# Partition counts of four kinds of DMA piece in a two-layer attention and long-convolution kernel

## The chip, the cores and the metric

The kernel runs on one core of a Trainium2 chip. A core has five engines that follow their own instruction streams: TensorE (PE, with weight loads listed as PEld), VectorE (DVE), ScalarE (ACT), GpSimd (POOL) and SyncE (SP). SP computes nothing here; it issues most of the DMA transfers, one after the other, and the 16 DMA engines of the core carry them out. SBUF, the on-chip memory, has 128 partitions (rows); a transfer names a range of partitions and what lies in each of them. The metric is the device time of one execution in microseconds (us), lower is better.

## The reference, cut to what matters

The input x has 2048 positions of 512 channels. Two kinds of layer alternate, A, B, A, B, each added to x:

```python
x = x + _A_ref(_layernorm(x), A_wqkv, A_wo)
x = x + _B_ref(_layernorm(x), B_A_re, ..., B_Dskip)
# and the same two once more, with the same weights
```

Layer A is a sliding, dilated attention: with 32 heads of 16 channels, position s attends to the eight positions s, s-2, ..., s-14:

```python
W, dil = 8, 2
idx = pos[:, None] - off[None, :]                     # off = 0, 2, ..., 14
logits = jnp.einsum("bhsd,bhswd->bhsw", q, kg) * scale
attn = _softmax(jnp.where(mask, logits, -1e9), axis=-1)
o = jnp.einsum("bhsw,bhswd->bhsd", attn, vg)          # then o @ wo
```

Layer B is a long convolution of every channel with a filter K made from the parameters, done as a Fourier product:

```python
Kf = rfft(pad(K)); Uf = rfft(pad(u))
y = irfft(Uf * Kf)[:L] + u * Dskip
```

## The kernel before, in words

Positions are stored with p as partition and a as column: position 16 p + a, so that 128 partitions times 16 columns hold all 2048. The residual stream x lies in `x_sb` as 128 x 16 x 512 bf16.

**Values and their shifted rows.** `v_ext` has 30 columns of 512 channels. Columns 14 to 29 hold the values of the 16 columns a. A position that looks back past column 0 needs the value of a higher column one partition earlier, so columns 0 to 13 repeat columns 16 to 29 shifted down by one partition. DVE's multiply L476 (`pv_mult`, tile `pav`) then reads eight columns in steps of two in one instruction. In `core`, `v_proj(a)` (L399 to L412) computes a column of values; the even columns come first (`VROWS`). After column 14, and again after column 15, SP copies the seven even or the seven odd shifted columns, from 127 source partitions to the 127 partitions below. Each such copy is two transfers: 112 partitions (L407) and 15 partitions (L408), of 7 x 1 KB each. In the first layer the event `("v", 0)` or `("v", 1)` follows: it calls `x_load`.

**Residual rows.** `x_load` (L1471) brings x from HBM into `x_sb`, four columns at a time, 128 partitions of 4 KB. It is called for block 0 after the even shift and for blocks 1 to 3 after the odd shift of the first layer. The output weights' loads (L312) stand before the first call on SP; behind the second stand the filter table's loads (`k_half_load`, L1374 and L1390, in two halves) and the first layer's twiddle loads. TensorE's output projection (L510, `out_proj`) reads `x_sb`.

**Twiddle pieces.** Layer B is a two-step Fourier transform. Its second step (`f2`, L828) multiplies with a twiddle matrix per frequency. `w2` is a list of 32 tiles of 128 partitions x 4 matrices x 128 (1 KB a partition), loaded from `w2_dram`. Their place is the memory of the attention layer's keys and projection weights (tile `kT_ext`, `homes` in L210), so they can only be loaded once the attention has read these. `load_w2(part)` (L595) issues eight loads; the letter `W` of the order strings `CORE0` and `CORE1` calls it, four times in each layer. The class attribute `self.layer` is 0 in the first pass and 1 in the second.

**What SP issues behind them in the second layer.** `FftB.run` calls `pump` (L756 and L758, in `kf_read`), which loads the filter's spectrum from `kf_dram` in 16 portions of three transfers each into a ring of buffers. Portions 0 to 6 are loaded during the attention, 7 to 9 right after the twiddle pieces, and each of 10 to 15 when DVE's product L865 (`u_mult`, tile `t`) has freed a buffer. Portion 7's place lies in the tile `kT_ext`, and its load waits until all twiddle loads have landed. The products run in the order of the portions, and the inverse transform of the second half needs all of them.

The order of instructions on DVE, ACT, PE and SP is written out by hand in strings such as `CORE1` and `ORDER1`; each engine works strictly in its order. SP's transfers use eight completion semaphores in turn, so a transfer waits until the one eight before it has landed.

Of the kernel before, what the change touches and what calls it, by code (L numbers as in the profile page):

```python
# [199 lines left out]
class LayerA:  # L200
# [162 lines left out]
    def core(self, x_sb, u, lnp, order, ev, nprod=0):  # L363

        tc, nc, lnst, l = self.tc, self.nc, self.lnst, self.layer
# [7 lines left out]
        with ExitStack() as c2:  # L373
            big = c2.enter_context(tc.tile_pool(name=f"a{l}_big", bufs=1, reuse_waits="tile"))
            v = big.tile([P, NA + 14, D], BF16, name="v_ext")
# [15 lines left out]
            def pq_tile():  # L391
                return ps_q.tile([P, 512], F32, name="pq", tag="pq")
# [6 lines left out]
            def v_proj(a):  # L399
                pp = pq_tile()  # L400
                for dt in range(NDT):
                    nc.tensor.matmul(pp[:], lhsT=xnT[:, dt, a * P:(a + 1) * P],  # L402
                                     rhs=wv[:, dt, :], start=(dt == 0), stop=(dt == NDT - 1))
                nc.scalar.copy(v[:, 14 + a, :].rearrange("p (d h) -> p d h", h=H), pp[:].rearrange("p (h d) -> p d h", h=H))  # L404
                if a >= 14:
                    b = a - 14
                    nc.sync.dma_start(v[1:113, b:14:2, :], v[0:112, 16 + b:30:2, :])  # L407
                    nc.sync.dma_start(v[113:128, b:14:2, :], v[112:127, 16 + b:30:2, :])  # L408
                    if b + l == 0:
                        self.load_wo(big)  # L410
                    if ("v", b) in ev:
                        ev["v", b]()  # L412
# [134 lines left out]
            def calls(f, *args):  # L547
                return [lambda a=a: f(*a) for a in args]

            def logit(f):  # L550
# [8 lines left out]
            rows = [(a,) for a in (ROWS1 if l else ROWS0)]  # L559
            ops = dict(  # L560
                m=calls(mult, *qft[nprod:]), l=calls(logit(lsum), *qft[nprod:]),
                q=calls(q_proj, *qft[len(self.qT) * NDT:]), v=calls(v_proj, *((a,) for a in VROWS)),
                x=calls(mx, *blocks), e=calls(sub_exp, *blocks), r=calls(recip, *blocks), n=calls(norm_p, *blocks), T=calls(turn, *blocks[:ncol]),
                P=calls(pv_mult, *rows), O=calls(out_proj, *rows[:15]), t=calls(x_stats, (12,), (13,)),
                b=calls(u_begin, (0, 4, "act", "pool"), (4, 8, "act", "act"), (8, 12, "act", "act")),
# [28 lines left out]

    def load_w2(self, w2_dram, part):  # L595
        for c in range(8 * part, 8 * part + 8):
            self.nc.sync.dma_start(self.w2[c], w2_dram[:, c * 4:(c + 1) * 4, :])  # L597

    def w2_loads(self, w2_dram):
        part = iter(range(4))  # L600
# [795 lines left out]
def kernel(  # L1396
# [16 lines left out]
    nc = tc.nc  # L1413
# [3 lines left out]
    w2_dram = dram.tile([P, P, P], BF16, name="w2_dram")  # L1417
# [14 lines left out]
    x_v = A_x.rearrange("b (p a) d -> p (b a) d", p=P)  # L1432
# [11 lines left out]
    x_sb = xpool.tile([P, NA, D], BF16, name="x_sb")  # L1444
# [25 lines left out]

    def x_load(bs):  # L1471
        for b in bs:
            nc.sync.dma_start(x_sb[:, b * 4:(b + 1) * 4, :], x_v[:, b * 4:(b + 1) * 4, :])

    with tc.tile_pool(name="ctmp_g2", bufs=1) as g2tmp:
        gx, ga, gs = build_g2(nc, g2tmp, C["p21"], g2_dram, kp[:].rearrange("p q a r -> p (q a r)"))
        G = lambda f, h: lambda: f(h)
        K = lambda h, j: lambda: k_part(h, j)
        for h in range(4):
            gx(h)  # L1480
        angled = iter(range(4))
        ev = {("v", 0): lambda: x_load((0,)), ("v", 1): lambda: x_load((1, 2, 3)),
              "c": lambda: ga(next(angled)), "1": lambda: k_half_load(0), "6": lambda: k_half_load(1),
              "2": G(gs, 0), "3": G(gs, 1), "4": G(gs, 2), "5": G(gs, 3),
              "7": lambda: nc.scalar.preload_act_table_set(EXP_LN),
              "8": lambda: k_half_fix(0), "9": lambda: k_half_fix(1)}
        ev |= la.w2_loads(w2_dram)
        ev |= {c: K(i // 4, i % 4) for i, c in enumerate("ABCDEFGH")}
        late = la.core(x_sb, u, lnp, CORE0, ev, 3)
# [121 lines left out]
```

## Time and profile before

| | us |
|---|---|
| median of three runs (389.51 to 390.7) | 390.63 |
| profiled execution | 390.38 |
| its span, first to last instruction | 387.9 |
| DVE busy | 369.0 (95%) |
| ACT busy | 338.1 (87%) |
| PE busy | 320.9 (83%) |
| POOL busy | 63.4 (16%) |

The granted TensorE clock over the span is 0.941 of full speed. The DMA engines moved 54.15 MB, 140 GB/s in the mean.

How to read what is shown below. A page gives, for one profiled execution, the busy time of each engine, a chain of work that ended last, groups of instructions, and DMA issues with the median time from issue to landing. A timeline row has start, duration, engine, source line, operation, output<-inputs and a count; `SPq` is SP's queue, and the duration of a DMA row there is the time that SP spends on issuing, not the time of the transfer. When several like instructions follow each other they are merged into one row, whose duration reaches from the first start to the last end. A row by source line gives minimum, median and maximum duration in ns, then the first and last start. The waits view lists who waited for whom: total us, times, longest. A window row gives the busy time of PE, PEld, DVE, ACT and POOL in that stretch, the granted clock, the DMA engines' mean busy share and GB/s.

### The profile page before, as it was taken

To read this page: it belongs to the slowest core of one execution; us is meant where nothing else is said; L and a number is where in the kernel's file an instruction comes from. 1 tells how busy PE (TensorE), PEld (TensorE's weight loads), DVE (VectorE), ACT (ScalarE), POOL (GpSimd) and SP (SyncE) were. 2 spreads that over 40 slices of the span, in tenths; PEclk is the share of its full clock that TensorE was granted. 3 is DMA by queue.
4 is the path that set the end of the run, shared out by engine and by line. 5 is a ranking of instruction groups with operands and counts; after the bars stand their busy time and mean duration, and the time that the engine had idled before them with its cause. 6 is when DMAs were issued, how large, how long until landed. Compare 5 with 4: busy or idle time off the path is not lost.

```text
span 387.9 us, 14510 instructions
## 1 busy us (share of the span) xinstructions
PE 320.9 (83%) x6312; PEld 220.8 (57%) x6361; DVE 369.0 (95%) x439; ACT 338.1 (87%) x581; POOL 63.4 (16%) x97
## 2 busy tenths in 40 slices
PE   3000277999999999999998999999999999997895
PEld 2000125757634455666887899553446676667895
DVE  6999999999999999999999989979999999989985
ACT  7999999898578799999999998865575889989994
POOL 9400980000190000101622200300000010000000
PEclk9555569999999999999999999999999999999999
DMA  7951822214026556487476733068305675003706
GB/s 208 398 178 17 86 74 68 43 29 88 25 71 172 153 183 191 107 232 214 183 276 240 272 113 111 3 230 259 96 0 136 189 211 167 4 3 106 224 25 196
DMA packets 68301, 54.15 MB, mean 140 GB/s; under 512 B 33545, under 2 KB 58670, under 8 KB 67982
## 3 DMA queue, kind: packets, MB, share of 16 engines
q1 hardware_dynamic: 66566, 48.70, 43.0%
q0 software_dynamic: 1664, 4.52, 3.2%
q8 instruction: 49, 0.80, 0.9%
q14 instruction: 14, 0.11, 0.1%
q10 hardware_dynamic: 8, 0.00, 0.0%
HBM read 30.15 MB, written 13.24 MB: 112 GB/s over the span
## 4 chain that ended last, share of the span: by engine, by line
PE 41%; ACT 22%; issue 4%; SPq 3%; DMA 2%; DVE 0%; ACTq 0%
PE pq L402 7%; ACT a1s L810 5%; PE pq L227 5%; ACT ub L877 5%; PE pp L286 3%; PE L L354 3%; PE po L501 3%; PE pq L512 2%; PE pb L821 2%; ACT xnT L195 2%; PE pb L891 2%; SPq L597 2%; PE pb L895 2%; PE pb L940 2%; PE L L428 2%
## 5 line engine op out<-in xcount | busy, mean ns | idle before, releaser
L476 DVE TENSOR_TENSOR pav<-attn,v_ext 128x4096 bf16<-128x4096 bf16 (+1 forms) x34 | 72.2, 2156 | 0.0
L346 DVE TENSOR_TENSOR prod<-qT,kT_ext 128x4096 bf16<-128x4096 bf16 x29 | 65.4, 2286 | 1.9 <-ACT qT L229 0.6
L1213 PE MATMUL pt<-ident,x_blk 128*128 128x128 bf16 x64 | 6.3, 241 | 40.1 <-ACT x_blk L195 40.1
L1127 DVE TENSOR_TENSOR A_t<-A_t,pow_t 128x1024 bf16<-128x1024 bf16 (+4 forms) x46 | 38.1, 868 | 0.1
L501 PEld LDWEIGHTS <-pav 64*128 64x128 bf16 x1984 | 31.1, 95 | 11.7 <-issue 5.8
L501 PE MATMUL po<-ident,pav 64*128 64x64 bf16 x1984 | 34.8, 190 | 0.3 <-issue 0.2
L512 PE MATMUL pq<-wop,oT 128*128 128x512 bf16 x120 | 31.3, 379 | 2.9 <-issue 2.1
L877 ACT CAST ub<-pb 128x1024 bf16<-128x1024 f32 x32 | 31.6, 1111 | 0.0
L828 PE MATMUL pb<-a1s,kT_ext 128*128 128x64 bf16 x768 | 27.7, 193 | 3.6 <-ACT a1s L810 1.9
L810 ACT CAST a1s<-pb 128x1024 bf16<-128x1024 f32 x30 | 29.4, 1052 | 1.4 <-PE pb L821 1.2
L402 PE MATMUL pq<-wv,xnT 128*128 128x512 bf16 x123 | 29.8, 379 | 0.3
L1223 PE MATMUL pp<-xnT,kT_ext 128*128 128x512 bf16 x89 | 25.5, 408 | 5.3 <-ACT kT_ext L1228 2.1
L1213 PEld LDWEIGHTS <-x_blk 128*128 128x128 bf16 x64 | 4.8, 108 | 42.4 <-ACT x_blk L195 41.2
L404 ACT CAST v_ext<-pq 128x512 bf16<-128x512 f32 x32 | 18.7, 587 | 11.1 <-PE pq L402 10.8
L828 PEld LDWEIGHTS <-kT_ext 128*128 128x128 bf16 x768 | 24.9, 98 | 6.0 <-issue 4.3
L1285 PEld LDWEIGHTS <-A_t 128*64 128x64 bf16 (+1 forms) x512 | 21.6, 103 | 3.8 <-DVE A_t L1127 0.2
L227 PE MATMUL pq<-xnT,kT_ext 128*128 128x512 bf16 x90 | 23.4, 380 | 0.4 <-issue 0.2
L1285 PE MATMUL pk<-B_t,A_t 128*64 128x84 bf16 (+1 forms) x512 | 23.5, 201 | 0.1
L810 DVE CAST a1s<-pb 128x1024 bf16<-128x1024 f32 x18 | 21.4, 1217 | 1.5 <-PE pb L821 1.1
L503 ACT CAST oT<-po 128x512 bf16<-128x512 f32 x31 | 17.8, 575 | 3.4 <-PE po L501 3.4
L402 PEld LDWEIGHTS <-xnT 128*128 128x128 bf16 x128 | 11.9, 98 | 15.5 <-issue 2.3
L512 PEld LDWEIGHTS <-oT 128*128 128x128 bf16 x128 | 12.5, 98 | 12.6
(262 smaller groups left out, 880.9 us busy)
## 6 DMA issues: line engine op xcount, KB each, us to landing
kT_ext<-w_dram SPq DMA_DIRECT2D x64, 128.0 KB, 3.5
w_dram<-xnT SPq DMA_DIRECT2D x1, 4096.0 KB
kf_ring<-kf_dram SPq DMA_DIRECT2D x13, 256.0 KB, 3.9
kf_ring<-kf_dram SPq DMA_DIRECT2D x26, 128.0 KB, 3.9
v_ext<-v_ext SPq DMA_DIRECT2D x4, 784.0 KB, 5.6
x_blk<-in_A_x_dram SPq DMA_DIRECT2D x4, 512.0 KB, 5.4
kT_ext<-in_A_wqkv_dram SPq DMA_DIRECT2D x4, 512.0 KB, 13.2
x_sb<-in_A_x_dram SPq DMA_DIRECT2D x4, 512.0 KB, 6.8
```

The lines of the kernel that those rows point to most:

```text
L227: nc.tensor.matmul(pq[:], lhsT=self.wqk[:, dt, ft * P:(ft + 1) * P], rhs=self.xnT[:, dt, q * 512:(q + 1) * 512], start=(dt == 0), stop=(dt ...
L346: nc.vector.tensor_tensor(pr, self.qT[q][:, ft].unsqueeze(1).to_broadcast([P, W, 4, P]), kap, ALU.mult)
L402: nc.tensor.matmul(pp[:], lhsT=xnT[:, dt, a * P:(a + 1) * P], rhs=wv[:, dt, :], start=(dt == 0), stop=(dt == NDT - 1))
L476: nc.vector.tensor_tensor(pv[:, i], attn[:, n % 4].unsqueeze(2).to_broadcast([P, W, DH // parts, H]), vap, ALU.mult)
L501: nc.tensor.matmul(po[:, h, 0, i * nt + ft, :], lhsT=pvf[rows, i, w, ft * P:(ft + 1) * P], rhs=ident[rows, rows], start=(w == 0 and ft + i ...
L512: nc.tensor.matmul(pw[:], lhsT=oT[:, ftp, :], rhs=self.wo[:, ftp, :], start=False, stop=(ftp == NDT - 1))
L810: (self.nc.scalar.copy if eng == "act" else self.nc.vector.tensor_copy)(dst, src)
L828: nc.tensor.matmul(p2[:, j, :], lhsT=self.w2[(ec * EC + j) // 4][:, j % 4, :], rhs=a1s[:, ec * EC + j, :], start=True, stop=True)
L877: nc.scalar.copy(ub[:], p2)
L1127: return lambda: nc.vector.tensor_tensor(*args)
L1223: nc.tensor.matmul(pps[kind, b, ft][:], lhsT=la.wqk[:, dt, c:c + P], rhs=la.xnT[:, dt, b * 512:(b + 1) * 512], start=(dt == 0), stop=(dt = ...
L1285: nc.tensor.matmul(o, lhsT=lhs, rhs=Bt[:, ri, c * CH + ql].rearrange("p b g -> p (b g)"), start=(not half and j % 4 == 0 and ri == 0), sto ...
```

## The change

Three places are changed. The shifted value rows go as 100 and 27 partitions instead of 112 and 15. In the second pass each twiddle tile is loaded as two pieces of 110 and 18 partitions instead of one of 128. The residual rows are loaded as 110 partitions per block, and the other 18 partitions once per call for all blocks of the call, so block 0 takes two transfers and blocks 1 to 3 take four. The bytes moved are the same.

```diff
-                    nc.sync.dma_start(v[1:113, b:14:2, :], v[0:112, 16 + b:30:2, :])
-                    nc.sync.dma_start(v[113:128, b:14:2, :], v[112:127, 16 + b:30:2, :])
+                    for lo, hi in ((1, 101), (101, 128)):
+                        nc.sync.dma_start(v[lo:hi, b:14:2, :], v[lo - 1:hi - 1, 16 + b:30:2, :])
...
     def load_w2(self, w2_dram, part):
         for c in range(8 * part, 8 * part + 8):
-            self.nc.sync.dma_start(self.w2[c], w2_dram[:, c * 4:(c + 1) * 4, :])
+            parts = (slice(0, 110), slice(110, 128)) if self.layer else (slice(0, 128),)
+            for p in parts:
+                self.nc.sync.dma_start(self.w2[c][p], w2_dram[p, c * 4:(c + 1) * 4, :])
...
     def x_load(bs):
         for b in bs:
-            nc.sync.dma_start(x_sb[:, b * 4:(b + 1) * 4, :], x_v[:, b * 4:(b + 1) * 4, :])
+            nc.sync.dma_start(x_sb[0:110, b * 4:(b + 1) * 4, :], x_v[0:110, b * 4:(b + 1) * 4, :])
+        rows = slice(4 * bs[0], 4 * bs[-1] + 4)
+        nc.sync.dma_start(x_sb[110:128, rows, :], x_v[110:128, rows, :])
```

## The prediction

> **What bounds the kernel now.** I read the page first (share of each engine, DMA issues), then SP's timeline, because the change only alters transfers that SP issues, then the DVE and weight-load timelines at the places that consume those transfers, and last SP's own waits.
>
> ```profile
> span 387.9 us, 14510 instructions
> ...
> PE 320.9 (83%) x6312; PEld 220.8 (57%) x6361; DVE 369.0 (95%) x439; ACT 338.1 (87%) x581; POOL 63.4 (16%) x97
> ...
> kT_ext<-w_dram SPq DMA_DIRECT2D x64, 128.0 KB, 3.5
> ...
> v_ext<-v_ext SPq DMA_DIRECT2D x4, 784.0 KB, 5.6
> ```
>
> DVE is busy 95% of the span, so in most stages it is the bound: a transfer that comes late to DVE costs its full lateness, one that comes in time costs nothing. The question is how much room each changed transfer has, and whether SP's queue, which works strictly in order, still has room behind them.
>
> The sum is made against the profiled execution: 390.38 us, of which 387.9 are the span and 2.5 lie around it. It stands 0.25 us below the median of three runs (390.63).
>
> **The shifted value rows.** SP's and DVE's timelines at the four shifts (two in each layer):
>
> ```profile
> 117.97 0.70 SPq L407 DMA_DIRECT2D v_ext<-v_ext  x1
> ...
> 130.04 0.64 SPq L407 DMA_DIRECT2D v_ext<-v_ext  x1
> ...
> 131.67 2.83 SPq L1473 DMA_DIRECT2D x_sb<-in_A_x_dram  x3
> ```
> ```profile
> 275.71 0.67 SPq L407 DMA_DIRECT2D v_ext<-v_ext  x1
> ...
> 292.17 0.64 SPq L407 DMA_DIRECT2D v_ext<-v_ext  x1
> ```
> ```profile
> 126.83 4.48 DVE L476 TENSOR_TENSOR pav<-attn,v_ext 128x4096 bf16<-128x4096 bf16 x2
> ...
> 139.08 2.28 DVE L476 TENSOR_TENSOR pav<-attn,v_ext 128x4096 bf16<-128x4096 bf16 x1
> ```
> ```profile
> 284.56 2.28 DVE L476 TENSOR_TENSOR pav<-attn,v_ext 128x4096 bf16<-128x4096 bf16 x1
> ...
> 301.23 4.49 DVE L476 TENSOR_TENSOR pav<-attn,v_ext 128x4096 bf16<-128x4096 bf16 x2
> ...
> 360.40 1.22 DVE L865 TENSOR_TENSOR t<-ub,kT_ext 128x2048 bf16<-128x2048 bf16 x1
> 361.54 2.35 DVE L865 TENSOR_TENSOR t<-ub,kx 128x2048 bf16<-128x2048 bf16 x2
> ...
> 364.94 2.35 DVE L865 TENSOR_TENSOR t<-ub,kf_ring 128x2048 bf16<-128x2048 bf16 x2
> ...
> 368.34 4.62 DVE L865 TENSOR_TENSOR t<-ub,kf_ring 128x2048 bf16<-128x2048 bf16 x4
> ```
> ```profile
> L408 SPq DMA_DIRECT2D v_ext<-v_ext x4: 898/932/963, 118.7 to 292.9; - x4
> ...
> DMA to landing us min/median/max: 5.1/5.3/5.5
> ```
>
> From the start of L407 to the multiply that reads the shift there are 8.86, 9.04, 8.85 and 9.06 us. Both pieces have landed after about 0.70 + 5.3 = 6.0 (L408 starts some 0.7 later), so each shift has 2.8 to 3.0 us to spare. What the copy does to the DMA engines shows in this window of the second layer, where little else moves:
>
> ```profile
> 278.00:279.00 1.00, 1.00 (x6) 0.42 (x5) 0.88 (x1) 0.98 (x2) 0.00 (x0) 1.00 0.96 260
> 279.00:280.00 1.00, 1.00 (x17) 0.55 (x15) 0.98 (x1) 0.76 (x2) 0.00 (x0) 1.00 0.99 295
> ```
>
> The last two columns are the DMA share and GB/s: 112 and 15 rows keep the 16 engines 96 to 99% busy. The 889 KB (784 + 105) take about 3.4 us of the 6.0 at 260 GB/s. How 100 and 27 rows spread, no row tells. Lower bound: as now. Upper bound: half the engines, 3.4 us more, and 9.4 is past all four dates by 0.4 to 0.6, in sum 1.9 us on DVE. I take nothing, since less than 2.8 of these 3.4 us is covered. [...]
>
> **The residual rows.** Four loads become six; the first pair stands in an idle stretch of SP before 130.04. In the second batch SP now needs 130.04 to 134.50 for five issues; six at L408's 0.93 plus 0.05 between two are 5.9, so SP comes out about 1.4 us later. If the engines' rate halved as well, the batch's 2.4 MB would take 8 us more, since the next queue entries wait for landings:
>
> ```profile
> SPq L1390 <- DMA x_sb<-in_A_x_dram: 3.2, 3, 2.0
> ```
> ```profile
> 182.09 0.37 SPq L1499 DMA_DIRECT2D g_sb<-g_dram  x1
> ...
> 189.52 1.17 SPq L853 DMA_DIRECT2D kT_ext<-kT_ext  x2
> ```
>
> SP runs without a pause through the filter loads and the first layer's twiddle loads and is first idle from 182.46 to 189.52: 7.1 us of room, which hides the 1.4. The upper end, 1.4 + 8, would overrun it by 2.3; the lower end is nothing. I take nothing, because the real spread must be much worse than the worst shift row to get there.
>
> **The second layer's twiddle pieces** are the large item: 32 loads become 64, behind one another in one queue.
>
> ```profile
> 301.34 16.72 SPq L597 DMA_DIRECT2D kT_ext<-w_dram  x29
> 320.64 0.52 SPq L756 DMA_DIRECT2D kT_ext<-kf_dram  x1
> ...
> 325.93 1.23 SPq L758 DMA_DIRECT2D kx<-kf_dram  x2
> 352.52 0.45 SPq L756 DMA_DIRECT2D kf_ring<-kf_dram  x1
> ...
> 363.30 0.54 SPq L756 DMA_DIRECT2D kf_ring<-kf_dram  x1
> 363.89 1.23 SPq L758 DMA_DIRECT2D kf_ring<-kf_dram  x2
> ```
> ```profile
> SPq L597 <- DVE prod L346: 4.6, 1, 4.6
> ...
> SPq L756 <- DMA kT_ext<-w_dram: 2.3, 1, 2.3
> ```
> ```profile
> 356.51 1.02 PEld L828 LDWEIGHTS <-kT_ext 128*128 128x128 bf16 x33
> ```
> ```profile
> L597 SPq DMA_DIRECT2D kT_ext<-w_dram x29: 320/430/1407, 301.3 to 317.6; - x29
> ...
> DMA to landing us min/median/max: 2.4/3.6/4.2
> ```
> ```profile
> L758 SPq DMA_DIRECT2D kf_ring<-kf_dram x12: 594/595/1452, 353.0 to 364.5; - x12
> ...
> DMA to landing us min/median/max: 2.6/3.7/5.5
> ```
> ```profile
> L407 SPq DMA_DIRECT2D v_ext<-v_ext x4: 637/654/699, 118.0 to 292.2; - x4
> ```
>
> Three loads go out early; the fourth waits 4.6 us for the last logit product and leaves at 301.34. From there 29 loads take 16.72 us, to 318.06. Now they are 58. Queued behind them on SP, in order: a wait for the last of them to land (320.64), nine filter loads for the seventh to ninth product (to 327.16), and six more triples that refill the ring for the tenth product and later ones. Today SP has 25 us of idle time before 352.52.
>
> How late may the twiddle loads end? Call the end E. The nine loads start at E + 2.6 and take 6.5. If SP is then behind, the six triples follow without a pause, 1.9 us each (363.30 to 363.84, 0.05, then 1.23, 0.05), so the last is issued at E + 20.6, its last piece starting 0.6 earlier and landing 3.1 after that (L758's pieces: 2.6 at least, 3.7 in the middle): E + 23.1. The last product starts at 368.34 + 3x1.15 = 371.8. So nothing is late while E stays under 348.7; past that each us of E costs a us. 58 loads from 301.34 reach 348.7 at 0.817 us each.
>
> The price of one piece decides. No row shows 110 or 18 rows. Lower bound: the 128-row load's 0.43 (0.48 with the gap), E = 329, cost nothing. 64-row pieces take 0.595 and 112 rows 0.654, while the 15-row piece, less data in the same form, takes 0.932: the issue is dear not by size but by the row count. Upper bound: twice the 15-row piece's extra (0.932 - 0.654 = 0.278) on top of the 64-row price, 1.15, or 1.20 with the gap: E = 370.9, cost 22.2 us. I take 0.932 + 0.05 = 0.98 for both, since 15 is the only count in the trace that isn't 16 or a multiple of it, as 110 and 18 aren't. E = 301.34 + 58x0.98 = 358.2, **9.5 us** past the date. The weight loads come in the same stretch: the last twiddle piece would land near 361 against its use about 357.4, 3.6 late, inside the 9.5 and not added. A gain from fewer bytes per engine at a time isn't excluded but has no path: everything that follows on SP has room today.
>
> [...]
>
> PE waits for two landings per twiddle tile instead of one: 32 more waits. Lower bound nothing, upper 32 times the 0.05 that a step between two issues costs on SP, 1.6 us; I take nothing, as PE stands idle in this stretch for other reasons. Bytes, matmuls, DVE and ACT work are unchanged.
>
> **Sum.** 390.38 + 0 (shifts) + 0 (residual rows) + 9.5 (twiddle queue) = 399.9 us.
>
> **Rivals.**
> - Not slower: the pieces are issued at 0.43 to 0.82 us. E stays under 348.7 and all is hidden, 390.4 us. It decides at 0.817 us a piece. For it: 128-row loads at 0.43. Against: the 15-row row. One piece at 0.43 and one at 0.93 would give 0.73 with the gaps, and so this case.
> - Dearer: odd counts cost more the further they are from 16. At 1.20 a piece the cost is 22.2, 412.6 us. For it: both new counts are further from a 16-way split than 15 is. Against: no row over 0.963 that isn't a stall.
> - The shifts bind: at half rate 1.9 us on DVE with twiddles hidden, 392.3. For it: the engines are full today. Against: 2.8 us of room.
> - Faster: the three residual loads behind L408 take 2.83 us where three at 0.43 would take 1.4, and this stall goes; 389.0 if all 1.4 came through, but SP has room there, so nothing waits for it.
>
> **How the numbers follow.** Forecast (0.90 to 1.08 a piece, 395 to 405 us) 0.45; dearer 0.25; hidden 0.17; shifts bind 0.07; faster 0.06. About 0.3% (1.2 us) is what a measurement of this kernel can tell from no change. Slower 0.45 + 0.25 + 0.07 = 0.77, same 0.17, faster 0.06. The range takes in the hidden case and reaches to the dearer price: 389.6 to 413, leaving out the faster case and the part of the dearer one beyond 1.20.
>
> **What would show it.** In the profile after: the two new twiddle pieces in SP's timeline at some 0.93 each and 58 of them ending near 358; the wait before the nine filter loads past 360; DVE idle before the products of the ring and the last of these some 9 us later; no idle time before the first multiplies with shifted rows; SP still idle before 189.5 in the first layer. The prediction is wrong if the pieces cost under 0.82 or well over 1, if DVE waits at a shift, or if SP's delay of the first layer shows on DVE.

## The result and the profile after

The changed kernel has a median of 393.86 us in 13 runs (391.53 to 401.06); the kernel before has 390.3 in 13 runs beside it. The ratio of the two is 1.0069, with a 95% interval of 1.0045 to 1.0094, which is 1.8 to 3.7 us and 2.7 in the middle. The median lies higher than the ratio says because four of the 13 runs (397.69 to 401.06) count as runs in a slower state and are left out of the ratio; the kernel before has none such in its 13, and what made these four slow is not shown. So the kernel became slower, as forecast, but by 2.7 us and not by 9.5, and, as the runs below show, for other reasons than the forecast gave.

The profiled execution of the changed kernel takes 394.72 us with a span of 393.0, against 390.38 and 387.9 before. That is 1.7 us above the 393.0 that the ratio gives (390.3 x 1.0069), so not every run can have lost all that this one profile shows. From its page: the span, DVE's busy time, the group of the multiply that reads the shifted rows, and the sizes of the new pieces.

```profile
span 393.0 us, 14575 instructions
...
PE 320.8 (82%) x6312; PEld 221.0 (56%) x6361; DVE 369.1 (94%) x439; ACT 338.4 (86%) x581; POOL 63.4 (16%) x97
...
L476 DVE TENSOR_TENSOR pav<-attn,v_ext 128x4096 bf16<-128x4096 bf16 (+1 forms) x34 | 72.2, 2158 | 1.1 <-DMA v_ext<-v_ext 1.1
...
kT_ext<-w_dram SPq DMA_DIRECT2D x32, 110.0 KB
...
v_ext<-v_ext SPq DMA_DIRECT2D x4, 700.0 KB
```

No engine has more work than before (DVE 369.1 against 369.0, PE 320.8 against 320.9); all that was added is waiting. The third line has something new: DVE stood 1.1 us before L476, waiting for a copy of shifted rows. The timelines of SP, then of DVE, of the changed kernel show the three changed places (line numbers behind the changed `load_w2` are two higher than before, those behind `x_load` four):

```profile
117.98 1.85 SPq L408 DMA_DIRECT2D v_ext<-v_ext  x2
...
130.06 1.75 SPq L408 DMA_DIRECT2D v_ext<-v_ext  x2
131.85 5.55 SPq L1475 DMA_DIRECT2D x_sb<-in_A_x_dram  x3
137.45 0.45 SPq L1477 DMA_DIRECT2D x_sb<-in_A_x_dram  x1
...
190.67 0.37 SPq L1503 DMA_DIRECT2D g_sb<-g_dram  x1
191.53 1.33 SPq L855 DMA_DIRECT2D kT_ext<-kT_ext  x2
...
297.95 32.38 SPq L599 DMA_DIRECT2D kT_ext<-w_dram  x64
332.02 0.51 SPq L758 DMA_DIRECT2D kT_ext<-kf_dram  x1
```
```profile
140.25 4.49 DVE L476 TENSOR_TENSOR pav<-attn,v_ext 128x4096 bf16<-128x4096 bf16 x2 [1.07 <-DMA v_ext<-v_ext]
```

The 64 twiddle pieces, the large item of the forecast, went out in 32.38 us, waits for the attention's last reads among them, and ended at 330.3. The last 58, the number that the forecast counted with, show the price of a piece:

```profile
305.36 24.96 SPq L599 DMA_DIRECT2D kT_ext<-w_dram  x58
```

That is 0.43 us each with the gap. The nine filter loads followed at 332.02, well before the date of 348.7. Nothing was lost there.

What was lost shows when each DVE instruction is set against the same one before, by the start times in DVE's timelines. The table gives how much later it starts (us), for the changed kernel and for the kernels of the experiments below, each in its one profiled execution. The columns are named by the instruction's start before: 139.08 is the first multiply with odd shifted rows in the first layer, 155.03 a maximum in that attention, 181.52 and 198.77 are PSUM evictions of the first Fourier transform (L810), 301.23 is the multiply with odd shifted rows in the second layer, 368.34 the last group of products.

| | 139.08 | 155.03 | 181.52 | 198.77 | 301.23 | 368.34 | span |
|---|---|---|---|---|---|---|---|
| changed kernel | 1.17 | 1.18 | 2.01 | 4.28 | 4.03 | 3.57 | 393.0 |
| shift_alone | 0.80 | 0.81 | 0.71 | 1.59 | 1.50 | 2.52 | 390.4 |
| resid_alone | 0.00 | 0.00 | -0.01 | -0.01 | -0.30 | -0.45 | 387.8 |
| twid_alone | 0.28 | 0.29 | 0.26 | 0.26 | -0.02 | -0.35 | 388.6 |
| resid_112 | 0.26 | 0.40 | 0.53 | 1.61 | 1.33 | 1.44 | 390.8 |
| even_all | 0.01 | 1.20 | 1.33 | 1.33 | 1.24 | 1.19 | 390.5 |
| shift_l2 | -0.01 | 0.00 | -0.01 | -0.01 | -0.19 | -0.01 | 388.9 |
| g_late | -0.01 | -0.01 | -0.01 | 3.15 | 3.26 | 3.95 | 393.2 |
| g_late_bit | 0.01 | 0.03 | 0.16 | 0.16 | -0.14 | -0.22 | 388.1 |
| after_g_pool | 0.48 | 0.49 | 1.09 | 2.04 | 2.36 | 2.22 | 391.6 |

In this profile the whole loss of the changed kernel up to the products arises in the first layer and the transform behind it, in two large steps (1.2 us at 139.08, 2.3 just before 198.77) and some small ones (0.8 in between). The second layer, where the forecast put all of it, added nothing. Between the last products and the end, the span of the changed kernel grows by another 1.5 us, but shift_l2, with the same code there as before, shows 1.0 and shift_alone none: one profile of that tail says nothing.

The first step is the wait in the timeline above. The second step is a stall of PE. PE's weight-load timeline at that place, first before, then changed:

```profile
194.98 1.37 PEld L821 LDWEIGHTS <-xnT 128*64 128x64 bf16 x48
196.44 1.01 PEld L828 LDWEIGHTS <-kT_ext 128*128 128x128 bf16 x32
```
```profile
196.98 1.37 PEld L823 LDWEIGHTS <-xnT 128*64 128x64 bf16 x47
200.57 0.11 PEld L823 LDWEIGHTS <-xnT 128*64 128x64 bf16 x1 [2.22 <-issue]
```

Before, 48 weight loads of L821 run through. Changed, 47 run, then PE stands 2.22 us before the 48th, and "issue" says that it waited for no semaphore and no engine. A look at the DMA queues in that place gives a hint; this is the DMA view of the changed kernel from 191.5 to 198, and then that of the kernel before from 189.5 to 196.2; both stretches begin with the swaps. Behind each queue stand its packets, MB and share of the 16 engines' time. `q8 instruction` is a queue of instruction packets, by their number those of PE (see the end):

```profile
DMA packets 664, 2.03 MB, mean 312 GB/s; under 512 B 102, under 2 KB 221, under 8 KB 536
...
q1 hardware_dynamic: 538, 1.60, 76.5%
q0 software_dynamic: 126, 0.42, 16.1%
```
```profile
DMA packets 567, 1.22 MB, mean 182 GB/s; under 512 B 112, under 2 KB 112, under 8 KB 566
...
q1 hardware_dynamic: 400, 0.66, 28.1%
q0 software_dynamic: 166, 0.55, 21.6%
q8 instruction: 1, 0.02, 1.1%
```

Before, the engines are half busy (28.1 + 21.6 + 1.1%) and a packet of instructions gets through. Changed, they are 93% busy for 6.5 us and none does. The next packet came at 198.1, 7.2 us after the one ahead of it (190.9), and PE went on 1.6 us after it had ended at 199.0. This is the DMA view from 198 to 199:

```profile
q8 instruction: 1, 0.02, 5.5%
```

What was added to the DMA engines in this stretch is the load of `g_sb` (1 MB), which SP issued at 182.09 before and at 190.67 now, 0.9 us ahead of the swaps of the filter spectra. That this load in this place is the cause was to be tested.

### The profile page after: what moved, and what is told of

The parts are those of the page before. It is cut to its first block, busy times and chain, and to the rows that moved or that the text cites. A ratio compares the mean times of both kernels' runs of the same rounds, so it can differ in the third digit from the quotient of the medians.

```text
span 393.0 us, 14575 instructions
## 1 busy us (share of the span) xinstructions
PE 320.8 (82%) x6312; PEld 221.0 (56%) x6361; DVE 369.1 (94%) x439; ACT 338.4 (86%) x581; POOL 63.4 (16%) x97
## 4 chain that ended last, share of the span: by engine, by line
PE 41%; ACT 18%; DVE 5%; issue 4%; DMA 3%; SPq 1%; DVEq 0%; ACTq 0%
PE pq L402 7%; PE pq L227 4%; PE po L501 4%; ACT ub L879 4%; PE pq L512 3%; PE pp L286 3%; PE pb L823 3%; ACT a1s L812 3%; PE L L354 2%; DMA v_ext<-v_ext 2%; ACT ln_junk L145 2%; PE pb L893 2%; ACT x_sb L518 2%; PE pb L897 2%; DVE pav L476 2%
## 5 line engine op out<-in xcount | busy, mean ns | idle before, releaser
L476 DVE TENSOR_TENSOR pav<-attn,v_ext 128x4096 bf16<-128x4096 bf16 (+1 forms) x34 | 72.2, 2158 | 1.1 <-DMA v_ext<-v_ext 1.1
L1287 PEld LDWEIGHTS <-A_t 128*64 128x64 bf16 (+1 forms) x512 | 21.6, 103 | 3.8 <-DVE A_t L1129 0.3
L823 PE MATMUL pb<-F1c,xnT 128*64 128x128 bf16 x256 | 17.1, 219 | 3.8 <-issue 2.1
```

Source lines behind the costliest of these rows:

```text
L476: nc.vector.tensor_tensor(pv[:, i], attn[:, n % 4].unsqueeze(2).to_broadcast([P, W, DH // parts, H]), vap, ALU.mult)
L823: nc.tensor.matmul(p1[half * 64:(half + 1) * 64, j, :], lhsT=lhs, rhs=m[:], start=True, stop=True)
L1287: nc.tensor.matmul(o, lhsT=lhs, rhs=Bt[:, ri, c * CH + ql].rearrange("p b g -> p (b g)"), start=(not half and j % 4 == 0 and ri == 0), sto ...
```

## The experiments

**One part at a time.** shift_alone has the first hunk of the change only, resid_alone the third, twid_alone the second.

> Only the shifted value rows are moved as 100 and 27; residual rows and twiddle pieces as before. Theory A (each shift now runs on about half of the DMA engines, and the DVE wait at the second shift of layer 1 needs the residual loads that run beside it in the same engines): the landing moves from about 6.0 us after L407's start to about 7.5, inside the 8.9 us of room, DVE waits at no shift, 390.0 to 391.0 us. Theory B (the shift alone is late): DVE waits 0.5 to 1.1 us before the first multiply with shifted rows at 139 us, 391.2 to 392.0 us.

> Only the residual rows are loaded as 110 and 18. Theory A (most of the loss is SP's lateness in layer 1, which moves the load of g_sb from 182 to about 190 us, on top of the swaps of the filter spectra, so that PE's instructions come late): SP issues the load of g_sb past 187, PE stands some 2 us with nothing waited for near 198, 392.0 to 393.5 us. Theory B (SP's idle time of 7 us hides it, as the prediction had it): 390.0 to 391.0 us.

> Only the twiddle pieces of the second layer are loaded as 110 and 18. Theory A (a piece costs SP about 0.5 us, as in the trace of the full change): the 64 pieces end near 330 us, all hidden, 390.0 to 391.0 us. Theory B (the smaller spread or the added waits of PE cost something that the full change's trace hides behind its other losses): 391.5 to 393 us.

Measured, as ratios to the kernel before with 95% intervals: shift_alone 1.0058 (1.0024 to 1.0091), resid_alone 1.0038 (1.0009 to 1.0066), twid_alone 1.0011 (0.9986 to 1.0035). Their sum is 1.07%, the full change has 0.69%; the intervals overlap. In us, by 390, they are 2.3, 1.5 and 0.4: against the 389.83 of the kernel before beside them, shift_alone's ratio gives 392.1, just past theory B's upper end, resid_alone's 391.3, between its two theories, and twid_alone's 390.3, within theory A. The twiddle pieces cost nothing that can be told, and the other two parts hold the loss. In twid_alone the 58 pieces start where the forecast had them start:

```profile
301.31 24.01 SPq L599 DMA_DIRECT2D kT_ext<-w_dram  x58
```

They take 0.41 us each and end at 325.3.

For the shift, theory B was right: shift_alone's DVE timeline has the wait without any change to the residual loads.

```profile
139.89 2.29 DVE L476 TENSOR_TENSOR pav<-attn,v_ext 128x4096 bf16<-128x4096 bf16 x1 [0.71 <-DMA v_ext<-v_ext]
```

For the residual rows the profiled execution shows no loss at all (389.69 us, the fastest of the 12 runs), and SP's waits and timeline show why it stands on the edge. Of resid_alone, waits first:

```profile
SPq L1390 <- DMA x_sb<-in_A_x_dram: 7.2, 4, 2.6
```
```profile
187.14 0.36 SPq L1501 DMA_DIRECT2D g_sb<-g_dram  x1
189.50 1.18 SPq L853 DMA_DIRECT2D kT_ext<-kT_ext  x2
```

SP comes out of the residual loads only 0.3 us later than before (134.88 against 134.55), but then waits 7.2 us for residual rows to land before it can go on with the filter rows (3.2 before), because the next transfers need the completion semaphores of those eight places back (in the traces of before and of the changed kernel all of SP's transfers, 279 and 313, take the same eight semaphores in turn). That lateness is carried through 47 us of unbroken issuing, and g_sb goes out at 187.14, 5.1 us later than before, 2.4 us before the swaps. Theory A's condition (past 187) holds, its stall near 198 is missing in this one execution, and the 12 runs (389.69 to 394.54) average 0.4% more. In shift_alone SP issues g_sb at the same 187.14, there with the slower shifts ahead of the residual loads: its three, unchanged, take SP 5.55 us to issue instead of 2.83. PE lost 0.7 us at 194. The two together make the 190.67 of the full change.

**Number of transfers or spread of rows.** resid_112 loads the residual rows in as many transfers as the change, but as 112 and 16 rows; even_all does that and also loads the second layer's twiddle pieces as 112 and 16, with shifts as before. From 130 to 142 us, with a shift and the residual rows under way, the DMA engines are 92.5% busy in even_all and 63.6% in the changed kernel.

```diff
+            nc.sync.dma_start(x_sb[0:112, b * 4:(b + 1) * 4, :], x_v[0:112, b * 4:(b + 1) * 4, :])
+        rows = slice(4 * bs[0], 4 * bs[-1] + 4)
+        nc.sync.dma_start(x_sb[112:128, rows, :], x_v[112:128, rows, :])
...
+            parts = (slice(0, 112), slice(112, 128)) if self.layer else (slice(0, 128),)
```

> The residual rows in as many loads as in the change, but as 112 and 16 rows, both of which can spread evenly over 16 engines. Theory A1 (the uneven spread of 110 rows makes SP late: the queue backs up behind the slow engines): SP comes out of the residual loads within 1 us of before (134.5), g_sb is loaded before 184 us, 390.0 to 391.0 us. Theory A2 (two transfers more in the queue make SP late whatever their rows): as with 110 and 18 rows, g_sb past 187 us, the same loss as that run within 0.5 us.

> The change's number of transfers with row counts that spread over 16 engines: shifts as 112 and 15, residual rows and the second layer's twiddle pieces as 112 and 16. Theory A (what costs is that 110, 18, 100 and 27 rows don't spread over all engines): 390.0 to 391.2 us, no DVE wait at a shift, SP out of the filter-row loads of the first layer at most 1.5 us later than before. Theory B (what costs is the larger number of transfers): 391.5 to 393.0 us.

resid_112 came out at 1.0023 (0.9995 to 1.005), even_all at 1.0039 (1.0024 to 1.0054), 391.75 us in the median against 390.3: even_all is slower, resid_112 can't be told from the kernel before or from resid_alone. So the number of transfers alone has a price: even_all's time lies in theory B's range, and SP came out of the first layer's filter rows 3.0 us later than before (165.39 against 162.41), past theory A's 1.5. In resid_112 g_sb goes out at 187.15, as A2 had it, although SP came out of the residual loads at 135.3. For A speaks that no DVE wait at a shift is left. How much of the change's 2.7 us is number and how much is spread, these runs don't settle. The loss of even_all's profiled execution is again one stall of PE with nothing waited for, at another place (146 us, in the output projection):

```profile
146.20 0.31 PEld L512 LDWEIGHTS <-oT 128*128 128x128 bf16 x2 [1.72 <-issue]
```

Here too an instruction packet was late: it came at 143.6, 16.5 us after the one ahead (in the kernel before at 140.1, 13.2 after), and PE went on 1.4 us after its end. The stretch of busy DMA engines ahead of it holds the residual and the filter rows.

**Is it the load of g_sb?** g_late is the kernel before, with that one load moved behind the first swap. `g` is the letter of the load in the order string, `kD` the first evicted spectrum, which triggers the swap.

```diff
-g KD KA KA KA KA KD KD KA KA KD KA kD KA KD ...
+KD KA KA KA KA KD KD KA KA KD KA kD g KA KD ...
```

> The kernel before, with nothing changed but the place of one load: g_sb (1 MB) is issued by SP behind the first swap of filter spectra (about 190 us) instead of at 182 us, which is where the full change has it because SP is 8 us late. Theory A (the collision of this load with the swaps delays PE's instruction packets and so PE): a gap of over 6.5 us between two instruction packets between 188 and 203 us, PE at L821 standing 1 to 2 us with nothing waited for, 391.0 to 392.5 us. Theory B (the 2 us that the full change lost there have another cause, or none that lasts): 389.5 to 390.5 us.

Ratio 1.0091 (1.0058 to 1.0124): 2.3 to 4.8 us from the place of a single load. The middle, 3.6, is more than the 2.7 of the whole change, though the intervals overlap, and it is above what theory A had put. The weight-load timeline of g_late, then its DMA view from 189.5 to 196.2:

```profile
194.96 1.31 PEld L821 LDWEIGHTS <-xnT 128*64 128x64 bf16 x46
198.66 0.11 PEld L821 LDWEIGHTS <-xnT 128*64 128x64 bf16 x2 [2.39 <-issue]
```
```profile
DMA packets 381, 1.58 MB, mean 236 GB/s; under 512 B 54, under 2 KB 54, under 8 KB 254
...
q1 hardware_dynamic: 301, 1.32, 68.7%
q0 software_dynamic: 80, 0.26, 10.5%
```

It is the fingerprint of the full change: the same run of 48 weight loads of L821, a stall of 2.39 us with nothing waited for, and no instruction packet in the 6.7 us ahead of it. The packet came at 196.3, 8.0 us after the one before, and PE went on 1.5 us after its end. Theory B is out.

But a moved load also changes SP's order and which transfer waits for which semaphore. g_late_bit leaves fifteen sixteenths of the load where it was and moves only the last sixteenth (64 KB), so that a transfer stands in g_late's place with hardly any of its bytes.

```diff
+        "g": lambda: nc.sync.dma_start(fb.g2[:, :, 0:15], g2_dram[:, :, 0:15]),
+        "h": lambda: nc.sync.dma_start(fb.g2[:, :, 15:16], g2_dram[:, :, 15:16])})
```

> As the run that moved the load of g_sb behind the first swap (+0.9%, 1.0091), but only a sixteenth of it (64 KB) is moved there; the other fifteen sixteenths are loaded at 182 us as in the kernel before, so that SP's order has one transfer more in the same place, with hardly any bytes. Theory A (the bytes of the load, queued in the DMA engines ahead of PE's instruction packets, are what delays PE): no gap of over 6 us between instruction packets after 188 us, no stall of 2 us at L821, 389.8 to 391.0 us. Theory B (the place in SP's queue does it, through the order of issues and the semaphores that the swaps wait for): PE stands 1 to 2 us there again, 392.0 to 395.0 us.

Ratio 1.0019 (0.9998 to 1.0041), and PE runs through at L821. The DMA view of the same stretch has its instruction packet again:

```profile
DMA packets 812, 1.25 MB, mean 187 GB/s; under 512 B 368, under 2 KB 368, under 8 KB 811
...
q1 hardware_dynamic: 651, 0.71, 32.1%
q0 software_dynamic: 160, 0.52, 21.0%
q8 instruction: 1, 0.02, 1.0%
```

So it is the megabyte in the DMA engines at this moment, not the order. That the stall itself is the wait for the instruction packet is read from the traces and wasn't switched on and off by itself. The dates speak for it: in the three stalls shown, of 1.72 to 2.39 us, PE went on 1.4 to 1.6 us after the end of a packet that had come 7.2 to 16.5 us after the one ahead. Smaller stalls of this kind are in other traces, 1.03 us at 193.81 in resid_112 and 1.44 us at 316.47 in shift_alone, each ending 1.4 to 1.6 us after a packet.

after_g_pool is the full change with this load issued by POOL, whose own queue is free:

```diff
-    fb.run(ORDER0, u, k=kp, late=[late[c] for c in LATE0.split()], more={"g": lambda: nc.sync.dma_start(fb.g2[:], g2_dram[:])})
+    fb.run(ORDER0, u, k=kp, late=[late[c] for c in LATE0.split()], more={"g": lambda: nc.gpsimd.dma_start(fb.g2[:], g2_dram[:])})
```

> The full change, with the load of g_sb issued by POOL, which stands idle until 185 us, so that it doesn't wait behind SP's late queue. Theory A (the late g_sb is most of what the residual rows and SP's lateness cost): g_sb leaves before 183 us, no stall of PE near 200, only the wait at the shift and small gaps remain, 391.0 to 392.0 us. Theory B (the place of g_sb is not what costs): as the full change, 392.7 to 394.0 us.

The stall of 2.2 us is gone from the profile: POOL issues the load at 180.05, and PE's 48 weight loads run through.

```profile
196.83 1.60 PEld L823 LDWEIGHTS <-xnT 128*64 128x64 bf16 x48
```

Yet the ratio is 1.0055 (1.0029 to 1.0081) against the change's 1.0069 (1.0045 to 1.0094): a gain of some half a microsecond that these intervals can't confirm, and 392.7 us in the median is the lower end of theory B's range. By the time alone theory A isn't confirmed. In this profile DVE waits for no odd shift, only 0.24 us for the first layer's even one, so the wait of 1.07 us isn't in every execution either. The table shows two steps behind it, 0.6 us up to 181.52 and 0.9 up to 198.77. The load now runs beside the twiddle loads that SP, still late, issues until 189.7. That this moves the collision and doesn't take it away is a reading of one profile.

**The shifts.** shift_l2 has the 100 and 27 rows in the second layer alone.

```diff
+                    for lo, hi in ((1, 101 if l else 113), (101 if l else 113, 128)):
```

> Shifted rows as 100 and 27 in the second layer alone, 112 and 15 in the first. Theory A (the second layer has room: the copy lasts to some 7.5 us after L407's start against 9 us of room, and little else moves there): DVE waits at no shift, 389.6 to 390.4 us. Theory B (the slower copy costs there too, as the gaps of the shift-alone profile near 318 and 340 us may say): 390.6 to 391.5 us.

Ratio 1.0007 (0.9976 to 1.0038) and no wait at a shift: theory A, and the forecast's own account of the second layer. One thing stays open: two of the runs in the ratio took 394.38 and 394.54 us, the other eight 389.55 to 390.7, and the profile is one of the eight. What the rows do to the engines shows in the 40 slices of the DMA share (tenths), in windows of equal length: before (275.5 to 285, the shift's first issue at 275.71), then the full change (279.5 to 289, first issue at 279.7).

```profile
DMA  0000003999999989999661000000000000000000
```
```profile
DMA  0000000365656556666956656443332210000000
```

The same 889 KB take 16 slices of 0.24 us before and 26 after, 3.8 and 6.2 us, at five to six tenths instead of nine. That the copy lasts longer isn't that SP issues it more slowly; the two issues take 1.79 us there and 1.67 before. From 282 to 286 us the share in the changed kernel is 0.51 to 0.69 in each us, what 8 to 11 of the 16 engines kept busy would give; which engines these are no view shows.

shift_31 goes further, with 96 and 31 rows in both layers.

```diff
+                    for lo, hi in ((1, 97), (97, 128)):
```

> Shifted rows as 96 and 31 in both layers. [...] Theory B (rows are dealt out over all engines whatever their number): as 112 and 15, DVE waits at no shift, 389.6 to 391.0 us.

408.93 us in the median, ratio 1.0459 (1.043 to 1.0489). Its DMA view over the second layer's even shift (285 to 302, both slices and GB/s) and DVE's waits:

```profile
DMA  0000000009999981200000000000000000000000
GB/s 0 0 0 0 0 0 0 0 12 272 214 226 263 301 268 60 65 24 22 24 24 24 24 24 24 24 24 24 24 24 24 24 24 27 24 24 24 17 0 0
```
```profile
DVE pav L476 <- DMA v_ext<-v_ext: 12.1, 3, 6.9
DVE pav L476 <- DMA k_rl<-kd_dram: 4.2, 1, 4.2
```

The 96 rows go at 214 to 301 GB/s; then the 31 rows trickle at 24, for 22 slices of 0.425 us, 9.4 us, at a share shown as 0, under a tenth. As an estimate from the 16 engines that is one: one of 16 kept busy gives 0.06, two would give 0.13. In the changed kernel a whole us with 0.06 stands beside 20 GB/s (287 to 288, the end of the even shift). DVE waited 6.9 and 5.1 us at the even shifts of the two layers and 0.2 at the second layer's odd one; at the first layer's odd one it stood 4.2 us, which the profile puts down to a load of filter rows. Theory B is out, whose time ended at 391.0. What decides how many engines a row count gets no run shows. Measured is how busy they were: nine tenths with 112 and 15 rows and with 96, five to six tenths with 100 and 27, under a tenth with 31.

**Where the residual loads stand.** after_x_early is the full change and x_early the kernel before, each with all four residual blocks loaded behind the even shift instead of three behind the odd one.

```diff
-        ev = {("v", 0): lambda: x_load((0,)), ("v", 1): lambda: x_load((1, 2, 3)),
+        ev = {("v", 0): lambda: [x_load((0,)), x_load((1, 2, 3))],
```

> The full change, with all four blocks of residual rows loaded behind the first shift (118 us) instead of one there and three behind the second (130 us). Theory A (the second shift is late because the residual loads run beside it in the same 9 to 10 engines, and SP's lateness behind it is what later delays PE): DVE doesn't wait at 140 us, at most a little at the first shift (126.8 us), SP issues the load of g_sb before 186 us, 390.0 to 391.5 us. Theory B (the shift's slower spread alone makes it late, and SP's lateness has no part): the wait of about 1 us at 140 us stays, 392.5 to 394.0 us.

> The kernel before, with all four blocks of residual rows loaded behind the first shift. Theory A (SP's idle stretch from 124 to 130 us takes the three loads, so its queue runs some 3 us earlier and the load of g_sb stands further from the swaps): g_sb before 180 us, 389.3 to 390.3 us, the same as before or a little better. Theory B (the three loads collide with the first shift and the wop loads instead): DVE waits 0.5 to 1.5 us at 126.8 us, 390.5 to 392.0 us.

Both theories on after_x_early were wrong: 398.9 us, ratio 1.0206 (1.0178 to 1.0234), slower than the change itself. Its DVE timeline, then SP's:

```profile
145.82 4.50 DVE L476 TENSOR_TENSOR pav<-attn,v_ext 128x4096 bf16<-128x4096 bf16 x2 [5.91 <-DMA v_ext<-v_ext]
```
```profile
130.05 6.06 SPq L408 DMA_DIRECT2D v_ext<-v_ext  x2
```

The wait at the odd shift grew from 1.07 to 5.91 us. The two pieces of the shift, 1.75 us to issue in the change, take 6.06. SP had issued the last residual rows, now ahead of them, at 128.88 us, and from 130 to 142 us the DMA engines were 71.3% busy; why SP stands in the issue no view shows. Nor does any show the "same 9 to 10 engines" of theory A: in the changed kernel the share from 130 to 139 us is 0.56, what 9 of 16 kept busy would give, and which they are stays open. x_early, with the same order but 128-row loads and 112 and 15 rows, costs nothing: ratio 1.0001 (0.9985 to 1.0018), no wait at a shift. So the early order is harmless as such; with the uneven counts the shift that SP issues next pays, with 6.06 us of issuing and a wait of 5.91. Which of the counts, those of the residual rows or of the shifts, does it wasn't separated. No kernel here beats the one before.

## Why the prediction was right or wrong

The direction was right and the size and the reason were not; since the cost that it named is absent, the right direction was luck. Point by point, by its own steps:

- **The twiddle pieces** (the step that failed): "I take 0.932 + 0.05 = 0.98 for both, since 15 is the only count in the trace that isn't 16 or a multiple of it". Measured, 24.01 / 58 = 0.41 a piece in twid_alone and 0.43 in the full change, so the end E is 325.3 and 330.3 instead of 358.2 and the 9.5 us are nothing; twid_alone has 1.0011 (0.9986 to 1.0035). What the change lost in place of it are waits of the first layer and the transform behind it: DVE's at the odd shift and PE's for late instructions. The dates were sound: by the forecast's own threshold, 0.817 us a piece, this is its rival "not slower". The error was to carry the price of a 15-row piece of a copy within SBUF (15 x 7 runs of 1 KB) over to loads from HBM with one run a row: in the changed kernel the copies within SBUF, of 100 and 27 rows, took SP 0.80 to 0.98 us each, the loads of 110 and 18 rows 0.43 with the gap. The nearest row for those was the 128-row load at 0.43, which the forecast showed and took as the lower end.
- **The shifted rows**, "I take nothing": in the profile of the changed kernel right for three of the four shifts, wrong for the odd one of the first layer, where DVE waited 1.07 us (0.71 in shift_alone). The spread was weighed in a window of the second layer "where little else moves", and there it holds (6.2 us instead of 3.8, and no wait). In the first layer the data arrived 140.25 - 130.06 = 10.2 us after the issue, past the room of 9.04. The upper bound, 9.4 us, was nearer than the value taken, and even it was short (by its own dates it costs 1.8 us in sum, not the 1.9 that it states).
- **The residual rows**, "SP comes out about 1.4 us later" and "7.1 us of room, which hides the 1.4": alone they come out only 0.3 us later; the 3.4 us of the full change (137.94 against 134.55) are the shift's doing, since shift_alone has nearly all of it (137.44). The cost lay in what the forecast had as its upper end and put at nothing, the landings that the next transfers wait for: 7.2 us in resid_alone and 7.1 in the full change instead of 3.2. At g_sb SP was 5.1 us late in resid_alone and 8.6 in the full change (190.67 against 182.09). The 8.6 pass the room of 7.1, so "SP still idle before 189.5" failed. But the first swap still came 0.5 us behind the load of g_sb on SP: SP's lateness was never charged as lateness on SP. It was charged as a megabyte moved on top of the swaps.
- **A missing step**: the forecast asked of each transfer who waits for its data. It did not ask what else the DMA engines carry. The instruction packets, read as PE's, come through the same engines (50 of them, 0.82 MB in the changed kernel), and a late transfer that nobody waits for can hold them up: with the load of g_sb on top of the swaps the next packet came 7.2 us (changed kernel) and 8.0 us (g_late) after the last. g_late shows the price of one load in the wrong place, 3.6 us (0.91% of 390.3, the interval 2.3 to 4.8).
- **The rivals**: "the shifts bind" (0.07) came nearest in time with 392.3, and its mechanism is there, at one shift in place of four. "Dearer" and the forecast's own range of 395 to 405 fell with the price of a piece. The wide range, 389.6 to 413, held the time by its width alone; none of its sums leads to 393.
- **What would show it**: of the list, the 0.93 a piece, the end near 358, the wait past 360 and the idle time before the ring's products are all absent; "if DVE waits at a shift" was named as what would make it wrong, and it does.

## What to carry to other kernels

Cost a transfer's issue from rows of its own form (memory to memory, runs per row) and not from a row count that looks alike. When rows are re-cut, look at how busy the DMA engines are while each count moves (here nine tenths with 112 and 15 rows, five to six with 100 and 27, under one with 31), and then at everything that is queued behind the copy: in shift_alone DVE waited 0.71 us for the slow piece, and SP came out of the residual loads behind it 2.9 us late. And when a queue runs late, ask not only which data comes late but which other traffic, the instructions among it, the delayed transfer will now run into.

## What the runs showed of the hardware

- Instruction packets move through the DMA engines: the changed kernel's page counts 50 of them on `q8 instruction` (0.82 MB, 16,384 bytes each in the trace) for 12,673 matmuls and weight loads, one for some 253. In the twelve longest pauses between two packets of the traces of before and of the changed kernel, 13.2 to 20.1 us, PE went through 230 to 364 of these, no more than in the other pauses (101 to 440 in 3.3 to 9.4 us), so the packets are read as PE's. When the engines were 79 to 93% busy for over 6 us, the next packet came 7.2 and 8.0 us after the last and PE stood 2.2 to 2.4 us, until some 1.5 us after the packet's end (the changed kernel and g_late).
- Run times scatter: in 35 runs the kernel before stays mostly within 389.3 to 390.3 but reaches 393.67, resid_alone spreads from 389.69 to 394.54 with one profile that lost nothing, and x_early's profile is 1.1 us late before its first changed transfer although its ratio is 1.0001. That late instruction packets make this scatter is argued, not shown; in any case a loss of this size can't be read from a single profile.
- A transfer of 31 rows moved at 24 GB/s where 96 rows moved at 214 to 301.
- SP can stand several microseconds in the issue of a small copy (6.06 us for two pieces that otherwise take 1.75) right behind residual rows in 110 and 18 partitions.
